# Block attention and soft mixture of experts: the score matmuls put into the four 64x64 parts of the array, and PSUM divided anew

## The chip, the cores and the metric

The kernel runs on one core of one Trainium2 chip. The metric is the device time of one launch in microseconds (us); lower is better. A difference of 0.2% is about what a measurement of this kernel can tell from no change.

## The reference

```python
def _attn_ref(q, k, v):                       # 8 batches, 8 heads, 576 rows, 64 columns, float32
    chunk = 64                                # 9 chunks: a query sees the keys of its own chunk only
    scores = scale * np.matmul(q_c, k_c.transpose(0, 1, 2, 4, 3))
    scores = scores - np.max(scores, axis=-1, keepdims=True)
    attn = np.exp(scores)
    attn = attn / (np.sum(attn, axis=-1, keepdims=True) + 1e-09)
    out = np.matmul(attn, v_c)

def _moe_ref(x, phi, w1, w2):                 # x: 4608 rows of 512; 8 experts of 4 slots, F = 1024
    logits = x @ phi                          # 4608 x 32
    d = softmax of logits over the rows
    slot_input = d.T @ x                      # 32 x 512, 4 slots to an expert
    slot_out = relu(slot_input[e] @ w1[e]) @ w2[e]
    c = softmax of logits over the slots
    return c @ slot_out
```

The two softmax lines are shortened; everything is float32.

## The kernel before

The kernel has two stages. The first (up to about 186 us) computes attention, the logits and the slot inputs. The second runs the experts and writes the output.

**Steps.** The first stage has 36 steps `t`, one for each pair of heads and each block of 512 rows (eight chunks); four steps make one block of all heads. Each step's work is spread over several turns of the loop, and the order of the code is the order on every engine: nothing reorders it. In turn `t` the loop records

- `s1(t)`: the scores. TensorE (PE) writes tile `psc`; VectorE (DVE) takes the row maximum (`mx`, L201) and subtracts it into `sc` (L203).
- every fourth turn (`t` = 7, 11, ... 31): `logits`, PE writes `pl`; `weights`, DVE takes the maximum (`rm`, `nm_run`), ScalarE (ACT) reads `pl` twice into `eT` and `lT`, then `al`.
- `transposes(t+2)`: PE turns queries and keys of a later step (`pqk`). ACT copies three quarters of them to `qkT` (L181), and DVE the last quarter (L179), which waits for ACT's three.
- in the turn after a logits turn: `partial`, PE writes `pp`, DVE adds it to `p_run`.
- `s3(t-3)`: PE turns `x` into `px`; DVE copies it to `xT` in odd turns, ACT in even ones.
- `s2a(t-1)`: PE turns the weights of attention into `pt`, ACT copies them to `at` (L218).
- in a logits turn: `natural`, PE turns `eT` and `lT` into `pe`; ACT copies `eN`, DVE reads it into `cm` and `c_all`.
- `s1b(t)`: ACT's exponential in place on `sc`.
- `s2b(t-2)`: PE multiplies with the values into `pav`; DVE divides (`rc`, and L243 into `x`).

So ACT's queue in a logits turn reads `eT`, `lT`, `al`, three `qkT` copies, `at`, `eN`, exponential; PE's reads `psc`, `pl`, `pqk`, `px`, `pt`, `pe`, `pav`. The turns that follow a logits turn are called the partial turn (`t` mod 4 = 0), turn 1 and turn 2 below; four turns are a period. Behind the loop the last steps are written out by hand, among them the four `s2b(32)` to `s2b(35)` close together, `logits(8)`, and `warm(n)`, which issues matmuls into a throwaway tile `pd`. The end of this part forms the slot inputs (`pst`).

**Scores.** Two heads lie one above the other on the 128 partitions of `qkT`. The keys are kept twice, each time with the other head's half zeroed, so that one matmul over all 128 rows of the array gives a chunk's scores of both heads (64 queries by 2x64 keys). There are eight such matmuls in a step.

**PSUM.** It has eight banks. Before, four single banks (`ps`) serve all of `psc`, `pl`, `px`, `pt`, `pe`, `pp` and `pd`, and two pairs of banks (`psp`) serve `pqk` and `pav`. A new tile waits until every reader of the bank's former tile is done. Which bank a tile gets is fixed when the program is built.

**Second stage.** `up` reads w1 and `down` w2; the output goes out in 18 halves (nine blocks, `h` = 0 and 1). The five w2 tiles of pool `wpb` lie in the memory of the first stage's tiles, and their loads wait until these are no longer read: `w2_2_0` lies over `qkT0` and `at0`, `w2_3_0` and `w2_4_0` over `xT`, `w2_5_0` and `w2_6_0` over `x0`. The loads stand in one queue (SP) in this order, the output behind them.

Of the kernel before, what the change touches and what calls it, by code (L numbers as in the profile page):

```python
# [16 lines left out]
def kernel(  # L17
# [69 lines left out]
    def load_w(pool, n):  # L87
        m, e, h = worder[n]
        t = pool.tile([P, 2048], F32, tag="w", name=f"w{m}_{e}_{h}") if pool else qk_w[n - NWA]
        if m == 1:  # L90
            t = t.rearrange("p (j f) -> p j f", j=2)
            nc.sync.dma_start(t, w1[e].rearrange("(j p) f -> p j f", p=P)[:, 2 * h:2 * h + 2])
        else:
            t = t.rearrange("p (g f) -> p g f", g=8)
            nc.sync.dma_start(
                t, w2[e].rearrange("(g p) f -> p g f", p=P)[:, :, DH * h:DH * (h + 1)])
        wt[m, e, h] = t

    with ExitStack() as actx:
        ap_ = actx.enter_context(tc.tile_pool(name="attn1", bufs=1))  # L100
# [25 lines left out]
        xb = tiles("x", [2, NHP, 2, P], range(2))
        xT = ap_.tile([P, 4, NF, P], F32, name="xT")
        v_sb = tiles("v", [4, 2, VW], range(NV))
        qkT.update(tiles("qkT", [3, BT], [1]))
        atb.update(tiles("at", [4, 2, CH], [1]))  # L130
# [26 lines left out]

        def transposes(u):

            pt = pair(f"pqk_{u}")  # L160
            for isq in range(2):
                src = qkn[(2 * u + isq) % NQK]
                for a in range(2):
                    for i in range(2):
# [1 line left out]
                        nc.tensor.transpose(  # L166
                            out=pt[:, 1 - isq, o:o + P], in_=src[:, a, P * i:P * (i + 1)], identity=ident)
            dst = qkT[u % 2]
            if batch[u // NHP] < B:
                pv = pt.rearrange("x s (a i g) -> x a s g i", a=2, i=2)  # L170
                dv = dst.rearrange("x s (g i j) -> x j s g i", i=2, j=2)
            else:
                pv = pt.rearrange("x s (a i g b) -> x a s b g i", a=2, i=2, b=B)
                dv = dst.rearrange("x s (b g i j) -> x j s b g i", b=B, i=2, j=2)
            for j in range(2):
                for a in range(2):
                    o = dv[D * a:D * (a + 1), j, 0:2 + a:1 + a]
                    if j == 1 and (a == 1 or u == 0):
                        nc.vector.tensor_copy(o, pv[D * j:D * (j + 1), a])  # L179
                    else:  # L180
                        nc.scalar.copy(o, pv[D * j:D * (j + 1), a])  # L181
# [1 line left out]
        ex = {}  # L183

        def s1(t):
            psc = bank(f"psc_{t}")
            qT, kb = qkT[t % 2][:, 0], qkT[t % 2][:, 1:3]

            pv = psc.rearrange("p (m a c x) -> p m c a x", m=2, a=2, c=2)
            for c in range(8):  # L190
# [2 lines left out]
                nc.tensor.matmul(  # L193
                    pv[CH * r2:CH * (r2 + 1), m, c2],
                    lhsT=qT[:, o:o + CH],
                    rhs=kb[:, :, o:o + CH],
                    start=True, stop=True,
                )
            pv = psc.rearrange("p (r x) -> p r x", x=CH)
            mx = a2.tile([P, 8], F32, tag="mx", name=f"mx_{t}")  # L200
# [11 lines left out]
        def s2a(t):  # L212
            sc = ex.pop(t).rearrange("p (r x) -> p r x", r=4)
            pt = bank(f"pt_{t}")
            for r in range(4):
                nc.tensor.transpose(out=pt[:, P * r:P * (r + 1)], in_=sc[:, r], identity=ident)  # L216
# [1 line left out]
            nc.scalar.copy(at.rearrange("p r g x -> p (r g x)"), pt)  # L218
            ats[t] = at

        def s2b(t):
            at = ats.pop(t)
# [4 lines left out]
            for i in range(4):
                m, a = divmod(i, 2)  # L230
                for c2 in range(2):
                    for r2 in range(2):
                        rs = slice(CH * c2, CH * (c2 + 1))
                        nc.tensor.matmul(  # L234
                            pav[CH * r2:CH * (r2 + 1), c2, i * VW:(i + 1) * VW],
                            lhsT=at[rs, i, r2, :],
                            rhs=v_sb[t % NV][rs, 2 * m + r2, a, :],
                            start=True, stop=True,
                        )
# [3 lines left out]
            nc.vector.tensor_tensor(  # L243
                xb[n % 2][:, :, hp].rearrange("p c m (a d) -> p c (m a) d", a=2),
                av[..., 0:D],
                rc.to_broadcast([P, 2, 4, D]),
                ALU.mult,
            )
# [442 lines left out]
```

## Time and profile before

| what | value |
|---|---|
| median of 3 runs | 252.47 us (252.29 to 252.5) |
| the profiled execution | 255.08 us; its span in the trace is 252.9 us |
| busy in the span | PE 87%, DVE 66%, ACT 59% |
| period of four turns in the loop | 19.03 us |
| first stage ends, second begins | 186.5 us |

Rows of the timeline read: start, duration, engine, line, operation, tile written <- tiles read, shape, count; in brackets the engine's idle time just before and what ended it. One matmul of float32 makes two records, so `x16` is eight matmuls; a transpose makes one.

### The profile page before, as it was taken

To read this page: it belongs to the slowest core of one execution; us is meant where nothing else is said; L and a number is where in the kernel's file an instruction comes from. 1 tells how busy PE (TensorE), PEld (TensorE's weight loads), DVE (VectorE), ACT (ScalarE), POOL (GpSimd) and SP (SyncE) were. 2 spreads that over 40 slices of the span, in tenths; PEclk is the share of its full clock that TensorE was granted. 3 is DMA by queue.
4 is the path that set the end of the run, shared out by engine and by line. 5 is a ranking of instruction groups with operands and counts; after the bars stand their busy time and mean duration, and the time that the engine had idled before them with its cause. 6 is when DMAs were issued, how large, how long until landed. Compare 5 with 4: busy or idle time off the path is not lost.

```text
span 252.9 us, 7897 instructions
## 1 busy us (share of the span) xinstructions
PE 220.7 (87%) x3205; PEld 164.3 (65%) x3205; DVE 167.9 (66%) x385; ACT 149.3 (59%) x300; POOL 7.1 (3%) x29
## 2 busy tenths in 40 slices
PE   6989887988988988988988988989999999998900
PEld 3777776767677677677677677666653356776900
DVE  4567886885995995995995995997471025754710
ACT  2497785786786686686686686675212115563600
POOL 1000000000000000000000000000022000000000
PEclk9999999999999999999999999999999999999765
DMA  6999998989989799999999788992499999999977
GB/s 192 336 291 249 308 307 222 313 272 245 277 186 309 188 322 256 309 334 309 334 333 323 193 288 241 304 290 74 148 346 348 348 347 349 348 365 326 350 239 247
DMA packets 88947, 71.87 MB, mean 284 GB/s; under 512 B 40784, under 2 KB 84816, under 8 KB 88912
## 3 DMA queue, kind: packets, MB, share of 16 engines
q1 hardware_dynamic: 88912, 71.38, 94.6%
q8 instruction: 25, 0.41, 0.7%
q14 instruction: 10, 0.08, 0.1%
HBM read 61.93 MB, written 9.44 MB: 282 GB/s over the span
## 4 chain that ended last, share of the span: by engine, by line
PE 49%; DVE 24%; ACT 16%; issue 4%; DMA 2%; SPq 0%; ACTq 0%; DVEq 0%
ACT qkT L181 13%; PE pf L620 7%; PE pqk L166 7%; PE psc L193 6%; PE po L585 6%; PE ph L555 6%; DVE qkT L179 6%; DVE x L243 5%; PE pav L234 4%; PE px L254 4%; PE pt L216 3%; DVE xT L259 2%; DVE mx L201 2%; PE pl L271 2%; DMA qk_w<-in_k_dram 2%
## 5 line engine op out<-in xcount | busy, mean ns | idle before, releaser
L181 ACT COPY qkT<-pqk 64x512 f32<-64x512 f32 x107 | 66.6, 622 | 31.5 <-PE pqk L166 29.7
L166 PE MATMUL pqk<-ident,qk_w 128*128 128x128 f32 x288 | 42.0, 292 | 6.1 <-DVE qkT L179 5.3
L166 PEld LDWEIGHTS pqk<-ident,qk_w 128*128 128x128 f32 x288 | 32.8, 147 | 15.3 <-DVE qkT L179 8.7
L179 DVE COPY qkT<-pqk 64x512 f32<-64x512 f32 x37 | 25.8, 697 | 23.8 <-ACT qkT L181 20.0
L193 PE MATMUL psc<-qkT 128*64 128x128 f32 x576 | 40.5, 284 | 0.4 <-DVE qkT L179 0.4
L193 PEld LDWEIGHTS psc<-qkT 128*64 128x64 f32 x576 | 31.7, 140 | 3.7 <-issue 1.1
L254 PE MATMUL px<-ident,x 128*128 128x128 f32 x144 | 22.8, 282 | 7.1 <-DVE x L243 6.5
L254 PEld LDWEIGHTS px<-ident,x 128*128 128x128 f32 x144 | 15.6, 140 | 18.0 <-DVE x L243 16.1
L234 PE MATMUL pav<-v,at 64*64 64x65 f32 x1152 | 25.3, 224 | 1.6 <-issue 1.3
L203 DVE TENSOR_TENSOR sc<-psc,mx 128x512 f32<-128x512 f32 x36 | 24.9, 691 | 1.3
L243 DVE TENSOR_TENSOR x<-pav,rc 128x512 f32<-128x512 f32 x36 | 24.9, 691 | 1.2
L234 PEld LDWEIGHTS pav<-v,at 64*64 64x64 f32 x1152 | 20.2, 134 | 7.5 <-issue 6.3
L201 DVE TENSOR_REDUCE mx<-psc 128x8 f32<-128x512 f32 x36 | 24.4, 677 | 0.3 <-PE psc L193 0.2
L216 PE MATMUL pt<-ident,sc 128*128 128x128 f32 x144 | 21.9, 275 | 1.5 <-ACT sc L208 1.5
L208 ACT ACTIVATE sc<-sc 128x512 f32<-128x512 f32 x36 | 23.0, 640 | 0.3 <-DVE sc L203 0.3
L218 ACT COPY at<-pt 128x512 f32<-128x512 f32 x36 | 21.2, 589 | 1.9 <-PE pt L216 1.5
L620 PE MATMUL pf<-sst,cst 128*128 128x256 f32 x72 | 18.7, 413 | 0.9 <-DVE sst L607 0.9
L620 PEld LDWEIGHTS pf<-sst,cst 128*128 128x128 f32 x72 | 17.4, 329 | 1.8 <-DVE sst L607 1.3
L216 PEld LDWEIGHTS pt<-ident,sc 128*128 128x128 f32 x144 | 16.6, 141 | 2.4 <-ACT sc L208 2.3
L626 DVE COPY ob<-pf 128x512 f32<-128x512 f32 x18 | 12.2, 690 | 4.0 <-PE pf L620 4.0
L624 ACT COPY ob<-pf 128x512 f32<-128x512 f32 x18 | 10.6, 587 | 6.9 <-PE pf L620 6.7
L555 PE MATMUL ph<-w,siT 128*32 128x512 f32 x128 | 14.4, 594 | 0.0
(90 smaller groups left out, 198.1 us busy)
## 6 DMA issues: line engine op xcount, KB each, us to landing
w<-in_moe_w_dram SPq DMA_DIRECT2D x30, 1024.0 KB
qk_w<-in_k_dram SPq DMA_DIRECT2D x32, 256.0 KB
qk_w<-in_q_dram SPq DMA_DIRECT2D x32, 256.0 KB
v<-in_v_dram SPq DMA_DIRECT2D x64, 128.0 KB
out_dram<-ob SPq DMA_DIRECT2D x16, 512.0 KB
qk_w<-in_moe_w_dram SPq DMA_DIRECT2D x2, 1024.0 KB
qk_w<-in_k_dram SPq DMA_DIRECT2D x8, 128.0 KB
qk_w<-in_q_dram SPq DMA_DIRECT2D x8, 128.0 KB
```

The source lines that it names most:

```text
L166: nc.tensor.transpose(out=pt[:, 1 - isq, o:o + P], in_=src[:, a, P * i:P * (i + 1)], identity=ident)
L179: nc.vector.tensor_copy(o, pv[D * j:D * (j + 1), a])
L181: nc.scalar.copy(o, pv[D * j:D * (j + 1), a])
L193: nc.tensor.matmul(pv[CH * r2:CH * (r2 + 1), m, c2], lhsT=qT[:, o:o + CH], rhs=kb[:, :, o:o + CH], start=True, stop=True,)
L201: nc.vector.reduce_max(mx, pv, axis=AX.X)
L203: nc.vector.tensor_tensor(sc.rearrange("p (r x) -> p r x", x=CH), pv, mx.unsqueeze(2).to_broadcast([P, 8, CH]), ALU.subtract)
L216: nc.tensor.transpose(out=pt[:, P * r:P * (r + 1)], in_=sc[:, r], identity=ident)
L234: nc.tensor.matmul(pav[CH * r2:CH * (r2 + 1), c2, i * VW:(i + 1) * VW], lhsT=at[rs, i, r2, :], rhs=v_sb[t % NV][rs, 2 * m + r2, a, :], sta ...
L243: nc.vector.tensor_tensor(xb[n % 2][:, :, hp].rearrange("p c m (a d) -> p c (m a) d", a=2), av[..., 0:D], rc.to_broadcast([P, 2, 4, D]), A ...
L254: nc.tensor.transpose(out=px[:, P * j:P * (j + 1)], in_=xb[n % 2][:, j % 2, hp, j // 2], identity=ident)
L555: nc.tensor.matmul(ph[SL * i:SL * (i + 1), :], lhsT=siT[:, j, :], rhs=wt[1, e, j // 2][:, j % 2, DM * h:DM * (h + 1)], start=(j == 0), sto ...
L620: nc.tensor.matmul(pf[:, DH * j:DH * (j + 1)], lhsT=cv[:, 2 * j2 + j, :], rhs=sst[h], start=True, stop=True)
```

## The change

The keys lose their zeroed copies: `qkT` holds keys and queries once, and four DVE memsets at the start go. A step's scores are sixteen matmuls, each over 64 rows of the array (one head, by rows) and 64 columns (one chunk of two neighbours, by columns), so that four of them use the four 64x64 parts of the array. The two heads' results lie in two banks, so `psc` takes a pair. PSUM is now three pairs, `pqk`, `psc` and `pav`, each with one buffer, and two single banks for `pl`, `px`, `pt`, `pe` and `pp`. Behind the loop, `bank` takes pairs apart into single tiles as their users end (`free`, `spare`); the halves of such a pair are one tile, which has the name of the first. The order of tiles in memory changes too.

```diff
-        ps = actx.enter_context(tc.tile_pool(name="ps", bufs=4, space=PSUM))
-        psp = actx.enter_context(tc.tile_pool(name="psp", bufs=2, space=PSUM))
+        ps = actx.enter_context(tc.tile_pool(name="ps", bufs=2, space=PSUM))
+        psp = actx.enter_context(tc.tile_pool(name="psp", bufs=1, space=PSUM))
+        spare = []
+        free = []
         def bank(name):
-            return ps.tile([P, 512], F32, tag="ps", name=name)
-        def pair(name):
-            return psp.tile([P, 2, 512], F32, tag="psp", name=name)
+            if free and not spare:
+                tag = free.pop(0)
+                free.append(tag)
+                if tag:
+                    t = pair(tag, name)
+                    spare.extend((t[:, 0], t[:, 1]))
+                else:
+                    spare.extend(ps.tile([P, 512], F32, tag="ps", name=f"{name}_{i}") for i in range(2))
+            return spare.pop(0) if spare else ps.tile([P, 512], F32, tag="ps", name=name)
+        def pair(tag, name):
+            return psp.tile([P, 2, 512], F32, tag=tag, name=name)
...
-        qkT = tiles("qkT", [3, BT], [0])
...
+        qkT = tiles("qkT", [2, BT], range(2))
+        xT = ap_.tile([P, 4, NF, P], F32, name="xT")
+        xb = tiles("x", [2, NHP, 2, P], [1])
+        v_sb = tiles("v", [4, 2, VW], range(NV))
         sc2 = ap_.tile([P, 2, DM], F32, name="sc2")
...
+        atb = tiles("at", [2, 2, 2, CH], range(2))
+        xb.update(tiles("x", [2, NHP, 2, P], [0]))
...
         def s1(t):
-            psc = bank(f"psc_{t}")
-            qT, kb = qkT[t % 2][:, 0], qkT[t % 2][:, 1:3]
-            pv = psc.rearrange("p (m a c x) -> p m c a x", m=2, a=2, c=2)
-            for c in range(8):
-                m, c2, r2 = c // 4, c // 2 % 2, c % 2
-                o = P * (2 * m + r2) + CH * c2
-                nc.tensor.matmul(pv[CH * r2:CH * (r2 + 1), m, c2],
-                    lhsT=qT[:, o:o + CH], rhs=kb[:, :, o:o + CH], start=True, stop=True)
+            psc = pair("psc", f"psc_{t}")
+            kT, qT = qkT[t % 2][:, 0], qkT[t % 2][:, 1]
+            for i in range(4):
+                m, c2 = divmod(i, 2)
+                for r2 in range(2):
+                    o = P * (2 * m + r2) + CH * c2
+                    for a in range(2):
+                        rs = slice(D * a, D * (a + 1))
+                        nc.tensor.matmul(psc[CH * r2:CH * (r2 + 1), a, CH * i:CH * (i + 1)],
+                            lhsT=qT[rs, o:o + CH], rhs=kT[rs, o:o + CH], start=True, stop=True)
...
-        for t in qkT.values():
-            nc.vector.memset(t[0:D, 2], 0.0)
-            nc.vector.memset(t[D:P, 1], 0.0)
...
         load_w(None, nw)
+        free.extend(('pqk', ''))
         t = NT - 1
...
         s2b(t)
+        free.extend(('psc', 'pav'))
```

In the loop no instruction changes its place; what changes is what each waits for. The next rows are PE's queue of the built program in logits turn 11 and partial turn 12, before, with the engines that a row waits for in brackets (`DMAHW` is a load).

```order
L216 MATMUL pt_10_901<-ident_63,sc2_95 128x128 [waits PE_49,Activation_49]
L309 MATMUL pe_1_907<-ident_63,eT_1_874 128x128 [waits Activation_49]
L234 MATMUL pav_9_917<-v1_100,at1_104 64x65 [waits DMAHW1_49]
L193 MATMUL psc_12_945<-qkT0_93 64x2x64 [waits PE_49]
L341 MATMUL pp_1_970<-x1_97,eN_1_910 32x512 [waits Activation_49]
L254 MATMUL px_9_976<-ident_63,x0_96 128x128 [waits DVE_49]
L216 MATMUL pt_11_982<-ident_63,sc2_95 128x128 [waits PE_49,Activation_49]
```

Here ACT's part in `pt_10` and `pt_11` is the exponential, and in `pe_1` it is `eT`: each waits only for its input. The same rows after:

```order
L228 MATMUL pt_10_993<-ident_63,sc2_101 128x128 [waits PE_49,Activation_49]
L321 MATMUL pe_1_999<-ident_63,eT_1_966 128x128 [waits Activation_49]
L246 MATMUL pav_9_1009<-v1_98,at1_103 64x65 [waits DMAHW1_49]
L205 MATMUL psc_12_1037<-qkT0_93 64x64 [waits DVE_49]
L353 MATMUL pp_1_1070<-x1_96,eN_1_1002 32x512 [waits DVE_49,Activation_49]
L266 MATMUL px_9_1076<-ident_63,x0_104 128x128 [waits DVE_49,PE_49]
L228 MATMUL pt_11_1082<-ident_63,sc2_101 128x128 [waits Activation_49]
```

By the semaphores' values ACT's part is now another instruction: `pt_10` lies in the bank of `pl_1` and waits for ACT's `lT`; `pe_1` lies in the bank of `pt_10` and waits for ACT's copy `at` of it; `pt_11` lies in the bank of `px_9` and waits for ACT's copy `xT` of it. `psc_12` waits for DVE's subtraction of step 11, and `pp_1` for DVE's copy of `px_8`. Every later period has the same banks.

The second place is PE's queue behind the loop, where the last `s2b` follow each other. Before:

```order
L234 MATMUL pav_33_2705<-v1_100,at1_104 64x65 [waits DMAHW2_49]
L234 MATMUL pav_34_2738<-v2_101,at0_94 64x65 [waits DMAHW6_49,PE_49]
L234 MATMUL pav_35_2763<-v3_102,at1_104 64x65 [waits DMAHW1_49,DVE_49,Activation_49]
L341 MATMUL pp_7_2789<-x1_97,eN_7_2760 32x512 [waits Activation_49]
L254 MATMUL px_34_2795<-ident_63,x0_96 128x128 [waits DVE_49,PE_49]
```

DVE's part in `pav_35` is `x` of step 33. After (the row that writes `pp_7` from `ident` and `x0` is `px_34`, in the other half of that pair):

```order
L246 MATMUL pav_33_2988<-v1_98,at1_103 64x65 [waits DMAHW2_49,DVE_49,PE_49]
L246 MATMUL pav_34_3020<-v2_99,at0_102 64x65 [waits DMAHW6_49,DVE_49,PE_49]
L246 MATMUL pav_35_3046<-v3_100,at1_103 64x65 [waits DMAHW1_49,DVE_49,PE_49]
L353 MATMUL pp_7_3071<-x1_96,eN_7_3043 32x512 [waits Activation_49]
L266 MATMUL pp_7_3071<-ident_63,x0_104 128x128 [waits DVE_49]
```

Each `pav` now waits for DVE's `x` of the step just before it, and `px_34` for DVE's `p_run`. In the same way the last `pd` of `warm(3)`, which shares a pair with `pm_8`, waits for DVE's `c_all`, and the second and fourth `pst` wait for ACT's copies of the first and third. At the start `pqk_1` waits for all four copies of `pqk_0`, where before it had a pair of its own; `pqk_2` and `pqk_3` now wait for those of the step just before theirs instead of the one before that. Among the loads, `w2_2_0` now lies over `qkT0` and `qkT1` and waits for `psc_35`; `w2_3_0` and `w2_4_0` wait for `pav_35`, `w2_5_0` for `pp_7` and `w2_6_0` for the last matmul that reads `xT`.

More of the change, by code (lines that the diff above doesn't have):

```diff
@@ L120, in tiles @@
             return {i: ap_.tile([P] + shape, F32, name=f"{name}{i}") for i in which}
-        qkT = tiles("qkT", [3, BT], [0])
-        atb = tiles("at", [4, 2, CH], [0])
+        qkT = tiles("qkT", [2, BT], range(2))
+        xT = ap_.tile([P, 4, NF, P], F32, name="xT")
+        xb = tiles("x", [2, NHP, 2, P], [1])
+        v_sb = tiles("v", [4, 2, VW], range(NV))
         sc2 = ap_.tile([P, 2, DM], F32, name="sc2")
[L126 to L130, printed above, removed]
+        atb = tiles("at", [2, 2, 2, CH], range(2))
+        xb.update(tiles("x", [2, NHP, 2, P], [0]))
         def load_qk(u):
@@ L158, in transposes @@
         def transposes(u):
-            pt = pair(f"pqk_{u}")
+            pt = pair("pqk", f"pqk_{u}")
             for isq in range(2):
@@ L166, in transposes @@
                         nc.tensor.transpose(
-                            out=pt[:, 1 - isq, o:o + P], in_=src[:, a, P * i:P * (i + 1)], identity=ident)
+                            out=pt[:, isq, o:o + P], in_=src[:, a, P * i:P * (i + 1)], identity=ident)
             dst = qkT[u % 2]
@@ L176, in transposes @@
                 for a in range(2):
-                    o = dv[D * a:D * (a + 1), j, 0:2 + a:1 + a]
+                    o = dv[D * a:D * (a + 1), j]
                     if j == 1 and (a == 1 or u == 0):
@@ L185, in s1 @@
         def s1(t):
-            psc = bank(f"psc_{t}")
-            qT, kb = qkT[t % 2][:, 0], qkT[t % 2][:, 1:3]
-            pv = psc.rearrange("p (m a c x) -> p m c a x", m=2, a=2, c=2)
-            for c in range(8):
-                m, c2, r2 = c // 4, c // 2 % 2, c % 2
-                o = P * (2 * m + r2) + CH * c2
[L193 to L200, printed above, removed]
+            psc = pair("psc", f"psc_{t}")
[6 more added lines that the diff above has]
+                        rs = slice(D * a, D * (a + 1))
+                        nc.tensor.matmul(
+                            psc[CH * r2:CH * (r2 + 1), a, CH * i:CH * (i + 1)],
+                            lhsT=qT[rs, o:o + CH],
+                            rhs=kT[rs, o:o + CH],
+                            start=True, stop=True,
+                        )
+            pv = psc[:, :, 0:4 * CH].rearrange("p a (r x) -> p a r x", x=CH)
+            mx = a2.tile([P, 2, 4], F32, tag="mx", name=f"mx_{t}")
             nc.vector.reduce_max(mx, pv, axis=AX.X)
             sc = sc2[:, t % 2]
-            nc.vector.tensor_tensor(sc.rearrange("p (r x) -> p r x", x=CH), pv,
-                                    mx.unsqueeze(2).to_broadcast([P, 8, CH]), ALU.subtract)
+            nc.vector.tensor_tensor(sc.rearrange("p (a r x) -> p a r x", a=2, x=CH), pv,
+                                    mx.unsqueeze(3).to_broadcast([P, 2, 4, CH]), ALU.subtract)
             ex[t] = sc
@@ L217, in s2a @@
             at = atb[t % 2]
-            nc.scalar.copy(at.rearrange("p r g x -> p (r g x)"), pt)
+            nc.scalar.copy(at.rearrange("p a m r x -> p (a m r x)"), pt)
             ats[t] = at
@@ L224, in s2b @@
             rc = a2.tile([P, 2, 4, 1], F32, tag="rc", name=f"rc_{t}")
-            pav = pair(f"pav_{t}")
+            pav = pair("pav", f"pav_{t}")
             for i in range(4):
@@ L235, in s2b @@
                             pav[CH * r2:CH * (r2 + 1), c2, i * VW:(i + 1) * VW],
-                            lhsT=at[rs, i, r2, :],
+                            lhsT=at[rs, a, m, r2, :],
                             rhs=v_sb[t % NV][rs, 2 * m + r2, a, :],
```

## The prediction

> **What bounds the kernel now.** First the page's busy times and groups: PE is busiest, and the score group (`psc`, L193) is its second largest.
>
> ```profile
> PE 220.7 (87%) x3205; PEld 164.3 (65%) x3205; DVE 167.9 (66%) x385; ACT 149.3 (59%) x300; POOL 7.1 (3%) x29
> L193 PE MATMUL psc<-qkT 128*64 128x128 f32 x576 | 40.5, 284 | 0.4 <-DVE qkT L179 0.4
> L234 PE MATMUL pav<-v,at 64*64 64x65 f32 x1152 | 25.3, 224 | 1.6 <-issue 1.3
> ```
>
> A share of the whole span doesn't tell what paces the loop, so next the timelines of DVE and ACT over one period, with a window of DVE's stretch from turn 1's `qkT` copy to the logits turn's `nm_run`:
>
> ```profile
> 108.79 0.70 DVE L179 COPY qkT<-pqk 64x512 f32<-64x512 f32 x1
> ...
> 116.08 0.16 DVE L286 TENSOR_TENSOR nm_run<-rm,nm_run 128x1 f32<-128x1 f32 x1
> ...
> 118.98 0.69 DVE L179 COPY qkT<-pqk 64x512 f32<-64x512 f32 x1 [1.58 <-ACT qkT L181]
> ```
>
> ```profile
> 108.79:116.24 7.45, 6.79 (x123) 5.74 (x119) 7.04 (x15) 4.58 (x8) 0.00 (x0) 1.00 1.13 332
> ```
>
> ```profile
> 106.83 1.93 ACT L181 COPY qkT<-pqk 64x512 f32<-64x512 f32 x3 [1.20 <-PE pqk L166]
> ...
> 117.04 1.91 ACT L181 COPY qkT<-pqk 64x512 f32<-64x512 f32 x3
> 118.97 0.59 ACT L218 COPY at<-pt 128x512 f32<-128x512 f32 x1
> 119.46 0.27 ACT L313 COPY eN<-pe 128x128 f32<-128x128 f32 x1
> ...
> 120.91 1.94 ACT L181 COPY qkT<-pqk 64x512 f32<-64x512 f32 x3 [0.66 <-PE pqk L166]
> 122.88 0.59 ACT L261 COPY xT<-px 128x512 f32<-128x512 f32 x1
> ```
>
> The third column of the window is DVE: 7.04 of 7.45 us (the rest are the short gaps between instructions), so there DVE is full. Behind `nm_run` (end 116.24) ACT does its exponentials and three `qkT` copies, and DVE's next copy starts at 118.98. PE is in neither piece. PE's timeline beside it:
>
> ```profile
> 105.65 1.09 PE L166 MATMUL pqk<-ident,qk_w 128*128 128x128 f32 x8
> ...
> 113.98 1.08 PE L271 MATMUL pl<-xT,phi_sb 128*32 128x128 f32 x32
> ...
> 116.36 0.60 PE L216 MATMUL pt<-ident,sc 128*128 128x128 f32 x4
> 116.85 0.33 PE L309 MATMUL pe<-ident,eT 128*128 128x128 f32 x1
> ...
> 117.27 0.70 PE L234 MATMUL pav<-v,at 64*64 64x65 f32 x32
> 117.89 1.09 PE L193 MATMUL psc<-qkT 128*64 128x128 f32 x16
> 119.73 1.09 PE L166 MATMUL pqk<-ident,qk_w 128*128 128x128 f32 x8 [0.75 <-DVE qkT L179]
> ...
> 122.50 0.60 PE L216 MATMUL pt<-ident,sc 128*128 128x128 f32 x4
> 123.03 0.70 PE L234 MATMUL pav<-v,at 64*64 64x65 f32 x32
> ```
>
> ```profile
> 133.01 1.08 PE L271 MATMUL pl<-xT,phi_sb 128*32 128x128 f32 x32
> ```
>
> From `pl` to `pl` a period is 133.01 - 113.98 = 19.03 us. PE runs ahead: in the logits turn it has done `pe` and `pav` by 118, and then waits 0.75 for DVE.
>
> **Scores.** A `psc` takes 1.02 us from its start to the next group's. Sixteen matmuls of 64x64 with 64 columns are nearest to `pav`, sixteen of 64x64 with 65 columns: 117.27 to 117.89, 0.62. I take 0.62; the ends are 0.5 (somewhat better, since neighbours here change the row half each time) and 1.02 (nothing gained). Where DVE and ACT pace the loop, the 0.40 is worth nothing; it enters only where PE comes on the path. [...]
>
> **The banks, in the loop.** I follow the path after the change with the durations above (a group's price is from its start to the next start). Up to `nm_run` nothing new binds; `pt` in the logits turn now waits for `lT`, still ahead of its ACT copy. That copy, `at`, stands behind the three `qkT` copies and starts at 118.97 as before. But now `pe` waits for it, and behind `pe` PE's whole queue. From 118.97: `at` 0.59; hop to PE 0.07 (an estimate from the other hops here, 0.03 to 0.09, as from `pqk`'s end at 106.74 to ACT's 106.83); `pe` 0.42; `pav` 0.62; `psc` 0.62; `pqk` until ACT can start 1.18 (119.73 to 120.91); three copies 1.97 (120.91 to 122.88); `xT` 0.59; hop 0.07, since `pt` now waits for `xT`; `pt` 0.53; `pav` 0.62; `psc` 0.62; `pqk` 1.18; three copies until DVE's 1.96 (106.83 to 108.79). Together 11.04, so turn 1's DVE copy starts at 130.01 instead of 108.79 + 19.03 = 127.82. The DVE-full stretch of 7.45 and ACT's 2.73 to the next `at` follow unchanged: a period of 7.45 + 2.73 + 11.04 = 21.22, or 2.19 more. DVE's other way to that copy (`rc`, `x`, `cs`, `mx`, subtraction behind the second `pav`) comes out at 129.5 and is just covered. There are seven such periods. The first began so:
>
> ```profile
> 39.99 1.88 ACT L181 COPY qkT<-pqk 64x512 f32<-64x512 f32 x3
> 41.90 0.59 ACT L218 COPY at<-pt 128x512 f32<-128x512 f32 x1
> ```
>
> ```profile
> 51.67 0.69 DVE L179 COPY qkT<-pqk 64x512 f32<-64x512 f32 x1 [0.44 <-ACT qkT L181]
> ```
>
> 41.90 + 11.04 = 52.94, 1.27 more than 51.67. Sum: 6 x 2.19 + 1.27 = **14.4 us**; ends 12 (`psc` at 0.5, shorter hops) and 20 (`psc` at 1.02, twice in each period).
>
> **The start.** The `pqk` pair has one buffer, so each step is in series: PE transposes, three ACT copies, DVE's copy, next step.
>
> ```profile
> 6.26 2.01 PE L166 MATMUL pqk<-ident,qk_w 128*128 128x128 f32 x8 [0.51 <-DMA qk_w<-in_k_dram]
> 8.62 1.98 PE L193 MATMUL psc<-qkT 128*64 128x128 f32 x16 [0.35 <-DVE qkT L179]
> ...
> 12.43 1.33 PE L193 MATMUL psc<-qkT 128*64 128x128 f32 x16
> ```
>
> ```profile
> 7.06 1.42 DVE L179 COPY qkT<-pqk 64x512 f32<-64x512 f32 x2 [2.82 <-ACT qkT L181]
> ...
> 36.08 0.69 DVE L179 COPY qkT<-pqk 64x512 f32<-64x512 f32 x1
> ```
>
> DVE's first copies end at 8.48, so `pqk_1` starts at 8.62 instead of 6.26. PE's groups take 2.0 here and 1.1 later; they became fast after 8.62 to 13 without a gap. With gaps in every step they stay slow longer: a step costs 2.0 + 0.1 + 1.96 + 0.70 + 0.06 = 4.8, and DVE's copies come at 12.6, 17.4, 22.2 and 26.9, then every 3.9 with PE fast (4.1 where the path runs over `x` and `psc`). The copy of step 8 then starts at 42.8 instead of 36.08: **6.7 us**. If PE is fast from 15 us on, it is 4.8; ends 4 and 7.5. The four memsets that go lay in DVE's wait of 2.82 and are worth nothing.
>
> **Behind the loop.**
>
> ```profile
> 173.62 0.70 PE L234 MATMUL pav<-v,at 64*64 64x65 f32 x32
> ...
> 174.88 0.70 PE L234 MATMUL pav<-v,at 64*64 64x65 f32 x32 [0.31 <-ACT eN L313]
> ...
> 184.39 0.83 PE L115 MATMUL pd<-ident 128*128 128x128 f32 x6
> 185.06 1.31 PE L382 MATMUL pst<-wsel,p_run 128*128 128x32 f32 x8
> ```
>
> ```profile
> 174.09 0.69 DVE L243 TENSOR_TENSOR x<-pav,rc 128x512 f32<-128x512 f32 x1
> ...
> 177.23 0.75 DVE L351 SCALAR_TENSOR_TENSOR p_run<-p_run,al,pp 128x512 f32<-128x512 f32 x1 [0.38 <-PE pp L341]
> ...
> 185.72 0.29 DVE L325 TENSOR_TENSOR c_all<-pm,cm 128x128 f32<-128x128 f32 x1
> ```
>
> `psc_35` waits for the subtraction of step 34: 0.6 later. `pav_34` and `pav_35` ran without waiting for the `x` just before them; now each is followed by `rc` and `x` (0.07 + 0.44 + 0.69) before the next starts, and `pav_35` comes at about 177.4, 2.5 later. `px_34` behind `p_run` adds 1.0. `pd` behind `c_all` (end 186.01) puts `pst` at 186.75, 1.7 later, and the `pst` pairs add 0.4. Together 2.5 + 1.0 + 1.7 + 0.4 = 5.6, ends 3 and 6.
>
> **Loads and output.** The w2 loads run ahead of PE by what SP lets them:
>
> ```profile
> 174.42 0.37 SPq L95 DMA_DIRECT2D w<-in_moe_w_dram  x1
> ```
>
> ```profile
> 240.00:252.90 12.90, 0.58 (x3) 0.38 (x2) 1.07 (x2) 0.59 (x1) 0.00 (x0) 0.56 0.77 245
> ```
>
> From 240 the output alone fills 12.9 us at 245 GB/s, 3.16 MB; nine halves of 0.52 MB are 4.72, and the missing 1.56 at some 355 GB/s began at 235.6. Their first data came from PE at about 234. The new places in memory let `w2_2_0` start when `psc_35` is done (170) and the next two behind `pav_35`, some 5 us earlier against PE. So the backlog goes, and I take 1.6 us off; ends 0 and 3. The rest of the second stage is the same and moves as a whole.
>
> **Sum.** 6.7 + 14.4 + 5.6 - 1.6 = 25.1. The profiled execution took 255.08 (252.9 of it span), which gives 280.2; the median lies 2.61 below it, so **277.6 us**.
>
> **Rivals.**
>
> *Faster, because PE is the bound.* PE's 87% speaks for it: 36 x 0.40 = 14.4 us less, 238. Against it: DVE's full window and its 1.58 us wait for ACT close the period without PE. It decides if `pe` doesn't have to wait, that is if `at` of the logits turn were done by 116.85 instead of 119.56. Chance 0.04; 0.01 more for costs and gains that cancel to within 0.2%.
>
> *The scores gain nothing.* Row halves that don't overlap would leave `psc` at 1.02: 0.40 x 2 x 7 = 5.6 more in the loop, 283. `pav` overlaps its four parts in the same tiling; but there the column half changes first. Chance 0.12.
>
> *PE's clock falls in the new gaps.* In the logits turn PE would be busy 1.2 us of the 3.9 from 115.7 to 119.6. Were it then as slow as at the start (1.98 against 1.09), the 5.8 us of PE on the path in each period would come out up to double; with half of that, 7 x 2.9 = 20, 298. Against it: waits of up to 0.75 in this loop left it fast, but none as long is in the trace. [...] Chance 0.06.
>
> *The forecast*, 0.77, with 270 to 283 as its own range. Range for all: 269 (the low ends of start, loop and tail) to 285 (which takes in the scores rival); about 0.8 of the chances lie in it. Faster by over 0.2% (what a measurement can tell) 0.04, within it 0.01, slower 0.95.
>
> **What would show it.** `psc` groups of about 0.65 us; PE's `pe` and `pqk` waiting for ACT `at` and ACT `xT` as releasers, some 2 and 1 us each period; `pl` to `pl` 21.2; DVE's wait before L179 still 1.58 in the logits turn, with new ones of about 0.9 in the partial turn and 0.5 in turn 1; the first `pl` about 6.5 later; `pav` waiting for DVE `x` at the end; DMA idle less around 175 to 182 of the old scale. I would be wrong if the period stays near 19, or if PE's groups in the loop last 2.0.

## The result and the profile after

| | before | after |
|---|---|---|
| median of the runs | 252.49 us (252.29 to 253.31) | 290.09 us (286.63 to 292.37) |
| ratio | 1 | 1.137, 95% interval 1.131 to 1.142 |
| profiled execution; its span | 255.08; 252.9 us | 288.37; 286.6 us |
| first `pl`; seventh `pl` | 37.39; 152.05 | 40.90; 172.06 |
| first `ph` of the second stage | 186.50 | 218.16 |

Slower, as forecast, but by 14 to 15%, not 10%: 290.1 lies outside the range of 269 to 285. (The ratio is taken without the two runs of the changed kernel whose clock was lowest, 0.892 and 0.903 on the mean, which took 291.8 and 292.37; the others had 0.915 and 0.95.) The span grew by 33.7 us: 3.5 up to the first `pl` (predicted 6.7); 16.5 over the six periods between the first and the seventh `pl`; 11.65 from there to the first `ph`, the seventh period included; 2.9 in the first group of `ph`; and 0.8 less between PE's end and the last output (predicted 1.6).

First the groups of PE in the changed kernel (busy time and mean ns of one, then the idle time just before them and what ended it):

```profile
L176 PE MATMUL pqk<-ident,qk_w 128*128 128x128 f32 x288 | 45.3, 308 | 12.3 <-DVE qkT L189 12.2
L205 PE MATMUL psc<-qkT 64*64 64x64 f32 x1152 | 26.3, 233 | 3.4 <-DVE sc L215 2.9 <-issue 0.5
L228 PE MATMUL pt<-ident,sc 128*128 128x128 f32 x144 | 23.0, 284 | 11.5 <-ACT xT L273 6.4 <-ACT lT L303 4.6 <-ACT sc L220 0.4
L321 PE MATMUL pe<-ident,eT 128*128 128x128 f32 x9 | 3.2, 357 | 13.4 <-ACT at L230 13.1 <-ACT eT L301 0.3
```

The scores did get cheaper: 26.3 us instead of 40.5. PE's idle time grew by more: `pe` waits 13.1 us for ACT's `at`, `pt` 11.0 for `xT` and `lT`, `pqk` 12.2 for DVE. PE's timeline over the stretch that the prediction followed, logits turn and partial turn of one period, and the next two `pl`:

```profile
128.99 1.08 PE L283 MATMUL pl<-xT,phi_sb 128*32 128x128 f32 x32
...
132.50 0.66 PE L228 MATMUL pt<-ident,sc 128*128 128x128 f32 x4 [0.97 <-ACT lT L303]
135.05 0.33 PE L321 MATMUL pe<-ident,eT 128*128 128x128 f32 x1 [1.90 <-ACT at L230]
...
135.53 1.15 PE L246 MATMUL pav<-v,at 64*64 64x65 f32 x32
136.45 1.08 PE L205 MATMUL psc<-qkT 64*64 64x64 f32 x32
137.46 1.66 PE L176 MATMUL pqk<-ident,qk_w 128*128 128x128 f32 x8
...
141.77 0.66 PE L228 MATMUL pt<-ident,sc 128*128 128x128 f32 x4 [1.07 <-ACT xT L273]
142.36 0.70 PE L246 MATMUL pav<-v,at 64*64 64x65 f32 x32
142.88 0.65 PE L205 MATMUL psc<-qkT 64*64 64x64 f32 x32
...
151.26 0.62 PE L283 MATMUL pl<-xT,phi_sb 128*32 128x128 f32 x10
152.52 0.85 PE L283 MATMUL pl<-xT,phi_sb 128*32 128x128 f32 x22 [0.63 <-issue]
...
154.79 0.66 PE L228 MATMUL pt<-ident,sc 128*128 128x128 f32 x4
157.34 0.33 PE L321 MATMUL pe<-ident,eT 128*128 128x128 f32 x1 [1.89 <-ACT at L230]
...
157.71 0.70 PE L246 MATMUL pav<-v,at 64*64 64x65 f32 x32
...
172.06 0.95 PE L283 MATMUL pl<-xT,phi_sb 128*32 128x128 f32 x25
```

The waits are the ones foretold: `pe` 1.90 for `at`, `pt` 1.07 for `xT`. But `pav`, `psc` and `pqk` behind `pe` take 1.15, 1.08 and 1.66, while `pav` and `psc` seven us later take 0.70 and 0.65 (and `pqk` behind them 1.09). The granted clock in windows of one us says why (columns: window, its length, busy time of PE, PEld, DVE, ACT and POOL with the number of instructions; then the clock, the DMA share and GB/s):

```profile
132.00:133.00 1.00, 0.50 (x4) 0.42 (x4) 0.22 (x1) 1.00 (x5) 0.00 (x0) 1.00 1.00 360
133.00:134.00 1.00, 0.16 (x2) 0.00 (x0) 0.00 (x0) 0.95 (x3) 0.00 (x0) 1.00 1.06 406
134.00:135.00 1.00, 0.00 (x0) 0.00 (x0) 0.58 (x1) 0.98 (x2) 0.00 (x0) 1.00 0.98 362
135.00:136.00 1.00, 0.95 (x18) 0.67 (x22) 0.88 (x3) 0.37 (x3) 0.00 (x0) 0.63 0.85 292
136.00:137.00 1.00, 1.00 (x51) 1.00 (x47) 0.74 (x4) 0.43 (x1) 0.00 (x0) 0.50 0.18 60
138.00:139.00 1.00, 1.00 (x7) 0.88 (x5) 0.96 (x2) 0.00 (x0) 0.00 (x0) 0.67 0.89 199
139.00:140.00 1.00, 1.00 (x10) 0.16 (x8) 0.19 (x1) 0.77 (x2) 0.00 (x0) 1.00 0.46 50
```

From 135.3 to 138.7 the clock is at one half (0.50). Five of the six periods have such a stretch and last 21.8 to 22.3 us; the sixth has none and lasts 172.06 - 151.26 = 20.80. So without the slow stretches the bank waits alone give a period a little under the predicted 21.22.

**Where the clock falls.** All edges of the clock in the trace lie on one grid: their distances are multiples of 3.413 us. The next table takes windows of this grid: the share of the window in which PE was busy, and the clock of the window behind it, in the changed kernel:

```
window from   PE busy   clock of the next window
 43.1          0.29      0.5
 67.0          0.47      0.5
 87.5          0.22      0.5
107.9          0.67      1.0
111.4          0.49      0.5
131.8          0.25      0.5
155.7          0.53      1.0
176.2          0.45      0.5
189.9          0.47      0.5
213.8          0.55      0.5
```

In these rows each of the seven windows in which PE was busy 0.49 or less was followed by one at half the clock, and so was one at 0.55; those at 0.53 and 0.67 were not. In the period from 151.26 on PE stood still for 0.63 us inside `pl`, and `pt` (154.79) then had no wait for `lT` left. `pe` waited 1.89 as in the slow periods, but the emptiest window came to 0.53, and the clock stayed at 1.00.

### The profile page after: what moved, and what is told of

Its sections match the earlier page's. It is cut to its first block, busy times and chain, and to the rows that moved or that the text cites. A ratio compares the mean times of both kernels' runs of the same rounds, so it can differ in the third digit from the quotient of the medians.

```text
span 286.6 us, 9051 instructions
## 1 busy us (share of the span) xinstructions
PE 218.9 (76%) x3781; PEld 158.6 (55%) x3781; DVE 167.7 (59%) x381; ACT 150.1 (52%) x300; POOL 7.1 (2%) x29
## 4 chain that ended last, share of the span: by engine, by line
PE 52%; ACT 25%; DVE 15%; issue 3%; ACTq 0%
ACT qkT L191 20%; PE pqk L176 13%; PE pf L631 6%; PE ph L566 6%; DVE qkT L189 5%; PE po L596 5%; PE pav L246 5%; PE psc L205 3%; PE pt L228 2%; PE pp L353 2%; DVE sc L215 2%; DVE x L255 2%; DVE mx L213 2%; ACT at L230 2%; ACT xT L273 1%
## 5 line engine op out<-in xcount | busy, mean ns | idle before, releaser
L176 PE MATMUL pqk<-ident,qk_w 128*128 128x128 f32 x288 | 45.3, 308 | 12.3 <-DVE qkT L189 12.2
L189 DVE COPY qkT<-pqk 64x512 f32<-64x512 f32 x37 | 25.7, 696 | 42.3 <-ACT qkT L191 41.4
L176 PEld LDWEIGHTS pqk<-ident,qk_w 128*128 128x128 f32 x288 | 35.9, 157 | 18.5 <-DVE qkT L189 11.0
L228 PE MATMUL pt<-ident,sc 128*128 128x128 f32 x144 | 23.0, 284 | 11.5 <-ACT xT L273 6.4
L205 PE MATMUL psc<-qkT 64*64 64x64 f32 x1152 | 26.3, 233 | 3.4 <-DVE sc L215 2.9
L246 PE MATMUL pav<-v,at 64*64 64x65 f32 x1152 | 26.9, 235 | 1.2 <-issue 1.0
L246 PEld LDWEIGHTS pav<-v,at 64*64 64x64 f32 x1152 | 21.7, 144 | 7.9 <-issue 5.5
L205 PEld LDWEIGHTS psc<-qkT 64*64 64x64 f32 x1152 | 22.7, 147 | 5.4 <-PE pav L246 2.6
L266 PE MATMUL px<-ident,x 128*128 128x128 f32 x128 | 19.9, 278 | 6.2 <-ACT qkT L191 6.0
L266 PEld LDWEIGHTS px<-ident,x 128*128 128x128 f32 x128 | 13.9, 141 | 16.5 <-issue 8.5
L566 PE MATMUL ph<-w,siT 128*32 128x512 f32 x128 | 17.2, 693 | 0.2 <-DVE s_rd L399 0.2
L637 DVE COPY ob<-pf 128x512 f32<-128x512 f32 x18 | 12.2, 690 | 4.0 <-PE pf L631 3.8
```

The lines of the kernel that those rows point to most:

```text
L176: nc.tensor.transpose(out=pt[:, isq, o:o + P], in_=src[:, a, P * i:P * (i + 1)], identity=ident)
L205: nc.tensor.matmul(psc[CH * r2:CH * (r2 + 1), a, CH * i:CH * (i + 1)], lhsT=qT[rs, o:o + CH], rhs=kT[rs, o:o + CH], start=True, stop=True,)
L246: nc.tensor.matmul(pav[CH * r2:CH * (r2 + 1), c2, i * VW:(i + 1) * VW], lhsT=at[rs, a, m, r2, :], rhs=v_sb[t % NV][rs, 2 * m + r2, a, :], ...
L266: nc.tensor.transpose(out=px[:, P * j:P * (j + 1)], in_=xb[n % 2][:, j % 2, hp, j // 2], identity=ident)
L566: nc.tensor.matmul(ph[SL * i:SL * (i + 1), :], lhsT=siT[:, j, :], rhs=wt[1, e, j // 2][:, j % 2, DM * h:DM * (h + 1)], start=(j == 0), sto ...
```

## The experiments

The times are medians; each ratio is to the kernel before, run beside it on the same chip (252.7 to 253.5 us).

**1. Filling the waits, too much** (`e1_fill`).

```
+ logits turn, ahead of pt: 5 x matmul(out=pav[:, 0, 260:388], lhsT=ident, rhs=ident)
+ logits turn, ahead of pe: 10 x the same
```

> The changed kernel, and in each logits turn 15 more matmuls (128x128 by 128 columns of the identity, 0.136 us each by pqk's 1.09 for 8) into columns of the pav pair that nobody reads: 5 ahead of pt and 10 ahead of pe, where PE waited 0.97 us for ACT lT and 1.90 us for ACT at. They fit into the waits (0.7 and 1.4 us). Theory (bank waits in series, and on top PE's clock, which falls after those waits): the granted clock reads 1.00 all through the loop, pl to pl falls from 21.8-22.3 to 20.8 us (the one period that had clock 1.00 was 20.80), five to six periods by 1.2 and something behind the loop: 281 us, between 279 and 285. Rival A (bank waits alone; the low clock is a reading that costs nothing): pl to pl stays 21.8-22.3 and the time 287 to 292. Rival B (the scores in 64x64 parts themselves cost the time): as rival A.

Measured: 293.12 us, ratio 1.157 (1.149 to 1.164). By its time a miss for the theory, and above the rivals' 287 to 292 too, but the price of the filler was wrong. PE's timeline, the filler ahead of `pe`, and a place 40 us on:

```profile
69.24 2.40 PE L239 MATMUL pav<-ident 128*128 128x128 f32 x20
71.47 0.27 PE L329 MATMUL pe<-ident,eT 128*128 128x128 f32 x1
...
112.69 1.08 PE L291 MATMUL pl<-xT,phi_sb 128*32 128x128 f32 x14 [2.82 <-issue]
```

A matmul of the identity took 0.22 us (71.47 - 69.24 for ten), not the 0.136 of a transpose (`pqk`'s 1.09 for eight), so `pe` came after the wait's end. And PE stood still inside groups (2.82 us here) without a wait that the profile shows. The granted clock was 1.00 in this loop but for the two windows behind that standstill (0.50 from 111.8 to 118.6). Undecided; taken up again with cheaper filler in 5.

**2. The banks without the scores** (`e2_banks`).

```
- psc = pair("psc", ...), 16 matmuls of 64x64
+ psc = pair("psc", ...)[:, 0], the 8 matmuls with zero blocks; qkT in three thirds
```

> The changed kernel with the old scores: 128 rows with zero blocks, three thirds of qkT, one bank (the other bank of the psc pair stays empty), the banks split as in the change. Theory (the banks cost the time): nothing of the loss goes; psc takes 1.02 us instead of 0.57 from its start to pqk, twice on the path of each period, so pl to pl is 21.7 with the clock at 1.00 (20.8 + 0.9) and up to 23 where the clock falls: 286 to 299, 293 likeliest. Rival B (the 64x64 parts cost the time): back to pl to pl of 19 and 252 to 258 us. Rival A (bank waits alone): 21.7 throughout, 290 us.

Measured: 297.17 us, ratio 1.159 (1.147 to 1.171), `pl` to `pl` 23.14 on the mean of six (41.81 to 180.68). None of the loss goes away with the old scores. The new ones save time: on the mean 1.3 us a period (21.86 with them), though the execution profiled here, 299.35 us, was one of the longer ones. The one period here with the clock at 1.00 (111.79 to 133.77) took 21.98, beside 20.80 with the new scores, which makes 1.2. Rival B falls. PE's timeline in the last loop period has the same wait and, behind it, the clock at 0.50 (from 163.3 on):

```profile
162.72 0.33 PE L320 MATMUL pe<-ident,eT 128*128 128x128 f32 x1 [1.89 <-ACT at L229]
...
163.98 1.97 PE L204 MATMUL psc<-qkT 128*64 128x128 f32 x16
```

**3. Start and end eased** (`e3_ends`).

```
- pt = pair("pqk", f"pqk_{u}")
+ pt = pair("pav" if u in (1, 3) else "pqk", f"pqk_{u}")
- pav = pair("pav", f"pav_{t}")
+ pav = pair("psc" if t == NT - 2 else "pav", f"pav_{t}")
```

> The changed kernel with two places eased: pqk of steps 1 and 3 in the pav pair (idle until step 2's pav), and pav of step 34 in the psc pair, so that pav of step 35 doesn't wait for the x before it. The loop between is the same. Theory (one buffer per pair holds the start and the end): pqk_1 starts at 6.3 instead of 8.55 us, the first pl comes 1 to 3 us earlier than 40.90, and from the last pl in the loop to the first ph it is 1 to 1.5 us less than 46.1; in all 2 to 4.5 us less, 285 to 288 beside 290. Rival (PE's slow groups and the loads hold the start, DVE's and ACT's work the end): the first pl within 0.5 of 40.9, the end within 0.5, the time as the changed kernel's.

Measured: 283.22 us, ratio 1.118 (1.110 to 1.126), more than expected. From the timelines, the changed kernel's start, and then that of this one:

```profile
8.55 1.57 PE L176 MATMUL pqk<-ident,qk_w 128*128 128x128 f32 x8 [2.96 <-DVE qkT L189]
...
17.52 1.09 PE L176 MATMUL pqk<-ident,qk_w 128*128 128x128 f32 x8 [1.69 <-DVE qkT L189]
```

```profile
6.16 1.97 PE L176 MATMUL pqk<-ident,qk_w 128*128 128x128 f32 x8 [0.52 <-DMA qk_w<-in_k_dram]
...
35.49 1.08 PE L283 MATMUL pl<-xT,phi_sb 128*32 128x128 f32 x32
```

The first `pl` comes 5.4 us earlier, and 1.9 earlier than in the kernel before. The end gained only 0.4 (45.7 from the last `pl` to `ph`, not 46.1). The wait that was eased did go: the last two `pav` start 0.88 apart (196.76 and 197.64) instead of 1.99 (200.49 and 202.48). But this execution also stood still for 1.43 us inside `psc` (186.14), with no wait that the profile shows, where the changed kernel's stood still for 0.49 (190.23).

**4. The waits moved off PE's path** (`e4_order`).

```
+ px in one single, all others in the second
- natural(...) behind s2a in the logits turn        + natural(..., False) behind s1 of the next turn
- partial(...) behind transposes                    + partial(...) behind s1, a turn later
- c_all from pe's second half                       + shifted(...) (pm) behind s1, two turns after pe
```

> The changed kernel with the same pairs and two singles, but the waits for a single moved off PE's path: px always in one single and all others in the second; pe behind the next step's psc (its l half apart, one turn pair later, as pm), pp one turn later, behind psc. The work is the same, one small transpose apart. Theory (bank waits in series on PE's path, with the clock on top): pe's wait for ACT at is covered by pav and psc, pt's wait for ACT xT goes, and with shorter gaps the clock stays up: pl to pl 19.0 to 20.0 us, 12 to 17 us less over the loop, 273 to 279. Rival A without the clock: 20.0 to 21.0, 279 to 284. Rival B (the 64x64 parts cost): pl to pl above 21.5, 286 to 292.

Measured: 286.83 us, ratio 1.124 (1.113 to 1.134), `pl` to `pl` 21.45 on the mean, 21.02 in the last with the clock at 1.00. The gain is less than the theory or rival A allowed, and the time lies in the range of rival B, which experiment 2 rules out. The edit made waits of its own. PE's timeline in turn 2 of the last loop period:

```profile
166.18 0.66 PE L271 MATMUL px<-ident,x 128*128 128x128 f32 x4 [0.66 <-DVE x L260]
168.11 0.63 PE L233 MATMUL pt<-ident,sc 128*128 128x128 f32 x4 [1.28 <-ACT xT L278]
```

The trace names `xT`, but `pt` lies in the single that `pm` had, whose last reader, DVE's `c_all`, ended at 167.97, 0.14 ahead of `pt`. Inconclusive on the theory.

**5. Filling the waits with transposes** (`e5_fill2`).

```
+ logits turn, ahead of pt: 4 x transpose(out=pav[:, 0, 260:388], in_=ident)   (on e3_ends)
+ logits turn, ahead of pe: 8 x the same
```

> The kernel e3_ends (283.2 us, pl to pl 22.12 on the mean of its six loop periods), and in each logits turn 12 transposes of the identity (0.136 us each, not the 0.27 of the matmuls in e1_fill) into unread columns of the pav pair: 4 ahead of pt, 8 ahead of pe; they end 0.4 and 0.8 us before the waits do. Nothing else changes. Theory (bank waits, and half a clock whenever PE was busy under about half of a fixed window of 3.41 us): in the loop no window falls under half, the granted clock reads 1.00 there, pl to pl 20.6 to 20.8, 8 to 9 us less over six periods: 275 us, between 272 and 278. Rival A (bank waits alone): pl to pl 22 and 282 to 288. Rival C (PE's extra instructions cost as much as the clock gives, as in e1_fill, where PE stood still for 1 to 3 us inside a group without a wait that the profile shows): 280 to 285.

Measured: 275.78 us, ratio 1.085 (1.079 to 1.092), as the theory had it. PE's timeline of one period:

```profile
98.76 1.08 PE L291 MATMUL pl<-xT,phi_sb 128*32 128x128 f32 x32
...
102.29 0.66 PE L228 MATMUL pt<-ident,sc 128*128 128x128 f32 x4 [0.55 <-ACT lT L311]
102.78 1.04 PE L239 MATMUL pav<-ident 128*128 128x128 f32 x8
104.87 0.33 PE L329 MATMUL pe<-ident,eT 128*128 128x128 f32 x1 [1.05 <-ACT at L230]
...
105.23 0.70 PE L254 MATMUL pav<-v,at 64*64 64x65 f32 x32
...
119.58 1.08 PE L291 MATMUL pl<-xT,phi_sb 128*32 128x128 f32 x32
```

`pe` starts when `at` is done, as without the filler, but `pav` takes 0.70. The clock is 1.00 all through the loop; the periods are 20.35, 20.83, 20.82, 20.82, 20.80 and 20.83. Work that computes nothing saves 7.4 us beside `e3_ends`.

**6. A bank of their own for `pe` and `pp`** (`e6_pe_bank`).

```
+ if name[:2] in ("pe", "pp"): return ps.tile(..., tag="pe", bufs=1)    (on e2_banks: the idle bank of psc's pair)
```

> The kernel e2_banks (old scores, psc in one bank, pqk and pav one pair each, two singles; 297 us) with pe and pp in the bank that stood empty beside psc, and pqk of steps 1 and 3 in the pav pair. Theory (what the loop lost is the waits of pe and pt for a single): pe's wait for ACT at (1.9 us) and pt's for ACT xT (1.1 us) are gone, the clock stays at 1.00, pl to pl 19.0 to 19.6 as in the kernel before; the end stays a few us longer: 252 to 259 us. Rival D (one buffer for psc and for each pair paces the loop): pl to pl 20.5 to 22, 264 to 280.

Measured: 261.67 us, ratio 1.036 (1.032 to 1.040), 35 us less than `e2_banks` (3.7 of it up to the first `pl`, 38.09 instead of 41.81). The time lies between the expected 252 to 259 and the rival's 264 to 280, 2.7 above the one and 2.3 below the other; the periods decide. PE's timeline:

```profile
136.19 1.08 PE L289 MATMUL pl<-xT,phi_sb 128*32 128x128 f32 x32
...
139.91 0.27 PE L327 MATMUL pe<-ident,eT 128*128 128x128 f32 x1
...
155.51 0.75 PE L289 MATMUL pl<-xT,phi_sb 128*32 128x128 f32 x20
```

`pe` follows `pt` without a wait, and the period is 19.32. Five of the six periods take 18.75 to 19.36, as the theory had it and not the 20.5 to 22 of the rival. The other, 21.41 (95.52 to 116.93), had a standstill of 1.80 and a slow window (0.50 from 100.8 on); what is left over the kernel before lies mostly there and at the end (39.5 from the last `pl` to `ph`, instead of 34.45).

**7. One wait alone** (`e8_one_wait`).

```
  kernel before, logits turn:
- pe = bank(f"pe_{b}")
+ pe = pts[t]          # the tile of the pt just ahead
```

> The kernel before with one wait of the change and nothing else of it: pe goes into the bank of the pt just ahead of it, so that it waits for ACT's copy at. Theory: PE waits 1.9 us at pe in each logits turn, and pav, psc (1.02) and pqk behind it come 2.0 us later, 1.3 to 2 of which reach the next period; now and then a 3.41 us window falls under half busy and the clock halves for one window, 0.5 to 1 us more: pl to pl 20.3 to 21.8, seven of them, 262 to 271 us. Rival E (the wait alone is covered by slack, and only all the waits together cost): 252 to 256.

Measured: 265.08 us, ratio 1.041 (1.036 to 1.046). PE's timeline:

```profile
99.60 1.08 PE L272 MATMUL pl<-xT,phi_sb 128*32 128x128 f32 x32
...
105.16 0.33 PE L310 MATMUL pt<-ident,eT 128*128 128x128 f32 x1 [2.59 <-ACT at L219]
...
120.19 1.08 PE L272 MATMUL pl<-xT,phi_sb 128*32 128x128 f32 x32
```

The row of 105.16 is `pe`, under the name of the tile that it now shares. Its wait ends when `at` does, and the period is 20.59, 1.56 more than before, with the clock at 1.00. (The first period, with a slow window (0.50) from 42.3 on, took 21.72.) So this one wait is most of the 1.8 us that the whole change costs a period at full clock. What the other waits (`xT`, `lT`) add, the shorter scores nearly take back: with all waits and the old scores the one period at full clock took 21.98 (experiment 2), 1.4 more than here, and with the new scores 20.80. No run has the other waits alone.

**8. The new scores only at the start** (`e7_start`).

```
  kernel before, SBUF tiles in the order of the change:
+ steps 0 to 6: psc in a pair of banks, 16 matmuls of 64x64; four singles from step 7 on
```

> The kernel before, with the scores in 64x64 parts in a pair of banks only for steps 0 to 6, where neither pl nor pe nor pp needs a bank, and old scores in one of four singles from step 7; SBUF tiles in the order of the change. Theory (the parts themselves are faster and the banks are the whole price): the first pl at 35.5 us as in e3_ends instead of 37.4, pl to pl 19.03, the output's lead 0.8 us: 249.5 to 251.5 beside 252.5, ratio 0.990 to 0.996. Rival (the start is paced by loads and by ACT's copies): 252 to 253, the ratio within 0.2% of 1.

Measured: 253.27 us beside 252.79, ratio 1.002 (0.999 to 1.004): a miss, no difference. In the profiled execution the first `pl` is 1.4 us earlier (35.99 beside 37.39), but the twelve runs show no gain. The trace of the kernel before is of an execution of 255.08 us, 2.6 above its median, so the 1.4 need not come from the change.

**9. The old banks behind the loop** (`e9_tail`).

```
  on e5_fill2, behind the loop:
+ loop.close(); ps = tile_pool(bufs=4); psp = tile_pool(bufs=2); old scores for steps 34 and 35 (qkT in three thirds)
```

> The kernel e5_fill2 (275.8 us), but behind the loop the banks of the kernel before (four singles, two pairs in turn) and its scores for the last two steps. Theory (pairs and two singles cost it behind the loop too): from the last pl of the loop to the first ph 36.2 us instead of 44.87 (34.45 in the kernel before, and 1.8 for the period that is still in it), and the first ph group at a full clock, 7.1 us instead of 9.64: 11 us less, 264.6, between 262 and 267. Rival (ACT and DVE carry work out of the loop, whatever the banks): 42 to 45 us there, 271 to 276.

Measured: 269.24 us, ratio 1.062 (1.053 to 1.071), between the two. From the last `pl` of the loop (159.52) to `ph` 41.25 us instead of 44.87. PE's timeline:

```profile
177.69 1.97 PE L207 MATMUL psc<-qkT 128*64 128x128 f32 x16 [2.54 <-DVE x L289]
...
200.77 7.07 PE L608 MATMUL ph<-w,siT 128*32 128x512 f32 x64 [0.25 <-DVE s_rd L433]
```

The exchange of the pools itself waits 2.54 for `x`, and behind that empty stretch the clock is at 0.50 from 177.2 to 180.6, where `psc` takes 1.97 instead of 1.09; without both some 38 would be left (41.25 - 2.54 - 0.88, an estimate). The first `ph` group takes the full-clock 7.07. How much of the end is banks stays open, between 3.6 and some 7.

**10. The start's clock alone** (`e10_start`).

```
+ 9 transposes of the identity into the pav pair behind transposes(0) and behind s1(0), s1(1), s1(2)
```

> The changed kernel, and at the start alone 9 transposes of the identity behind the transposes of step 0, and 9 behind each of the first three psc, into the pav pair, which is idle then; the loop and the end are the changed kernel's. pqk_1 still waits for DVE's copy, until 8.5 us. Theory (of the 5.4 us that the pav pair saved at the start in e3_ends, over half were clock: PE stood idle from 5.6 to 8.5 us and was slow until 15.8): PE is fast from 9 to 10 us, and the first pl comes at 37 to 39 us instead of 40.9; 287 to 289. Rival (the pair's one buffer alone): the first pl at 40.4 to 41.4 and 289 to 292.

Measured: 289.46 us, ratio 1.148 (1.140 to 1.155). PE's timeline:

```profile
8.30 1.06 PE L176 MATMUL pqk<-ident,qk_w 128*128 128x128 f32 x8 [2.01 <-DVE qkT L189]
...
34.23 0.41 PE L205 MATMUL psc<-qkT 64*64 64x64 f32 x14
37.25 0.50 PE L205 MATMUL psc<-qkT 64*64 64x64 f32 x18 [2.61 <-issue]
...
41.45 1.08 PE L288 MATMUL pl<-xT,phi_sb 128*32 128x128 f32 x32 [0.71 <-ACT xT L278]
```

PE is fast from 8.3 us on (1.06 for `pqk`), but the first `pl` comes no earlier (40.90 in the changed kernel). The rows between say why. Up to the `psc` at 34.23 this kernel is 1.5 us ahead of the changed one, where the same group starts at 35.77. Then PE stands still for 2.61 us inside the group, with no wait that the profile shows, and the lead is gone. So the slow clock cost some 1.5 us at the start, not over half of the 5.4, as my theory had it; most of the 5.4 is the pair's one buffer. The times of the four runs don't show the 1.5, and whether they too stood still isn't in a trace.

**11 and 12. Less filler** (`e11_fill4`, `e12_fill8`): as in 5, but only ahead of `pe`, 4 or 8 transposes.

> The kernel e5_fill2 with 4 transposes ahead of pe in each logits turn (0.54 us) and none ahead of pt. In e3_ends, without any, five windows of 3.41 us in the loop had PE busy 0.29 to 0.49 of the time, and each was followed by one at half clock; no window at 0.55 or more in the loop was. Theory (the clock goes by PE's busy share in a fixed window, and about half is the edge): 0.54 us are 0.16 of a window, so the emptiest ones stay at 0.45 and still halve the clock, the others don't: two to four half-clock windows in the loop, its periods between 20.8 and 22.2, 278 to 283 us. Rival (any work in the long wait breaks it up, since it is the length of one gap that counts: 0.6 us and then 1.3): no half clock in the loop, 275 to 277.

> The same with 8 transposes ahead of pe (1.09 us, 0.32 of a window) and none ahead of pt. Theory: the emptiest windows come to 0.6, no half clock in the loop, pl to pl 20.8, 275 to 277 us, as with 12. Rival (the wait ahead of pt, 0.97 us, is enough to halve the clock): half-clock windows stay, 279 to 283.

Measured: 276.32 us (1.084 to 1.096) with 4 and 274.69 (1.068 to 1.089) with 8. With 8 no slow window is left in the loop, as expected. With 4 one is left, behind a window in which PE was busy 0.52 (102.3 to 105.7); the other windows of the loop, at 0.57 or more, have none behind them. That is fewer than the two to four expected. The times fit the rival; that a slow window remains fits the theory.

## Why the prediction was wrong in size

The mechanism held: single banks in short supply put `at` and `xT` into PE's path. The step that failed is a rival, "PE's clock falls in the new gaps", given a chance of 0.06: "waits of up to 0.75 in this loop left it fast, but none as long is in the trace". So the sum took every group of PE at its fast duration. In the loop after, the clock fell five times, behind waits for banks of at most 1.90 us. Their length alone does not tell: the wait of 1.89 at 157.34 (PE busy 0.53 of that 3.41 us window) left the clock at 1.00, and one of 1.89 at 178.13 (0.45 of its window) was followed by half the clock. Point by point, of the 33.7 us:

- *Start*, 6.7 predicted, 3.5 measured. The pair's one buffer was most of it: without it (experiment 3) the first `pl` comes 5.4 earlier, 1.9 ahead of the kernel before. The premise that PE stays slow with gaps in every step was wrong: it was slow until 15.8 (1.09 for `pqk` at 17.52, behind a gap of 1.69), which cost some 1.5 (experiment 10). The prediction's own figure for a PE that is fast from 15 us on, 4.8, was nearer.
- *Loop, bank waits*, 14.4 predicted. At full clock (experiment 5) the six periods take 124.45 us against 114.66, 9.8 more, and the seventh is taken at 1.8: 11.6. A period came out at 20.8 instead of 21.22 mostly because `pav` and `psc` take 0.52 and 0.57 from start to start there, not 0.62, and both are on the path twice. The rival by which the scores gain nothing fell with it.
- *Clock*, nothing predicted, 10.8 measured: 16.5 - 9.8 = 6.7 in the loop, 1.3 for each of five windows; 1.2 in the seventh period (from `pl` at 172.06 to `psc` at 189.09 17.03, in experiment 5 from 161.21 to 177.05 15.84); 2.9 in the first `ph` group (9.95 instead of 7.07, and 7.07 again in experiment 9). The 1.5 at the start and the slow window behind the loop are not in it. The rival's own price of 2.9 a period was about twice too high, since one window falls in a period, and not in every one.
- *Behind the loop*, 5.6 predicted, 8.6 measured (11.65 less 1.8 and 1.2). The waits that were named are there:

```profile
192.69 0.70 PE L205 MATMUL psc<-qkT 64*64 64x64 f32 x32 [1.02 <-DVE sc L215]
193.31 1.12 PE L266 MATMUL pt<-ident,x 128*128 128x128 f32 x4
...
199.63 0.66 PE L266 MATMUL pt<-ident,x 128*128 128x128 f32 x4 [0.78 <-ACT at L230]
...
202.48 0.69 PE L246 MATMUL pav<-v,at 64*64 64x65 f32 x32 [1.03 <-issue]
...
214.75 0.94 PE L126 MATMUL pm<-ident 128*128 128x128 f32 x6 [1.51 <-DVE c_all L337]
```

  The `pav` at 202.48, that of step 35, carries no releaser, but DVE's `x` of step 34 ended 0.11 ahead of it (201.68 + 0.69). Not named were a slow window from 193.3 on (`px`, in a pair under the name of `pt`, 1.12 instead of 0.66) and the wait for `at` at 199.63. That the rest is banks was argued, not shown (experiment 9).
- *Output*, -1.6 predicted, -0.8 measured.

The terms that were mis-sized add up to -3.2 - 2.8 + 10.8 + 3.0 + 0.8 = 8.6, less 0.4 that lay outside the span: the 8.2 us between the predicted 280.2 and the profiled 288.37. Without the 10.8 of the clock the forecast would have been 2.6 too high, and that near only by luck: start and loop were 6.0 too dear, end and output 3.8 too cheap.

## What to carry to other kernels

Here `psc` got a pair of banks, and the single banks went from four to two. Before splitting anew, find for each tile the last reader of the bank it would inherit, and where that copy stands in its engine's queue. One such wait (`pe` behind `at`) cost 1.56 of the 1.8 us that a period lost at full clock. And where new waits leave PE as idle as here, price the clock too: windows of 3.41 us in which PE was busy 0.22 to 0.49 were followed by half the clock, and throwaway transposes in the waits gave back 7.4 us.
